# Attention with a sliding window and a spectral mix: v loaded like q and k and transposed twice, 128 keys per score tile

## The chip, the cores and the metric

The kernel runs on one core of a Trainium2 chip. It is timed on the device, in microseconds (us); a measurement is the median of several runs. Before the change it takes 463.44 us, the median of 3 runs (461.84 to 464.57). A profiled execution of the same kernel is where all views come from; its span is 460.1 us. The engines are called as the profile calls them: PE (TensorE, with PEld for its weight loads), DVE (VectorE), ACT (ScalarE), POOL (GpSimd) and SP (SyncE, which here issues transfers).

## The reference

Two stages follow each other. The first is attention for 8 batches, 8 heads, 576 tokens and 64 columns a head, with a window of 128 tokens and a bias that falls with the distance (one slope a head). The second takes the attention's output as `x` (8 x 576 x 512), multiplies the first 64 modes of its Fourier transform along the tokens by a complex 512 x 512 matrix each, and adds a product with `w_ch`.

```python
def _attn_ref(q, k, v):
    scores = scale * np.matmul(q, k.transpose(0, 1, 3, 2))
    rel = pos[:, None] - pos[None, :]
    bias = slopes[:, None, None] * (-np.abs(rel).astype(np.float32))[None, :, :]
    mask = (rel >= 0) & (rel < window)
    scores = np.where(mask, scores + bias[None], -1000000000.0)
    scores = scores - np.max(scores, axis=-1, keepdims=True)
    attn = np.exp(scores)
    attn = attn / (np.sum(attn, axis=-1, keepdims=True) + 1e-09)
    return np.matmul(attn, v)

def _moe_ref(x, w_r, w_i, w_ch):
    X = np.fft.rfft(x, axis=1)
    Y = np.zeros_like(X)
    Xr, Xi = (np.real(X[:, :n_modes]), np.imag(X[:, :n_modes]))
    Yr = np.einsum('bmd,mde->bme', Xr, w_r) - np.einsum('bmd,mde->bme', Xi, w_i)
    Yi = np.einsum('bmd,mde->bme', Xr, w_i) + np.einsum('bmd,mde->bme', Xi, w_r)
    Y[:, :n_modes] = Yr + 1j * Yi
    u = x + np.fft.irfft(Y, n=S, axis=1)
    return u + np.maximum(u @ w_ch, 0.0)
```

Everything comes and goes as float32; the kernel computes in bfloat16 with float32 sums. The weights `w_r` and `w_i` are 64 x 512 x 512 each, 134 MB in all.

## The kernel before

**Units and slots.** A unit is one pair of heads (`s`, 0 to 3) of one batch (`b`): 32 units. The first group is pair 0 of all batches (units 0 to 7), the second is pairs 1 to 3 (units 8 to 31). The order of work on every engine is the order in which the program writes it (a manual schedule). `_slot(n)` writes one slot: the scores of unit n, the transposes of unit n+1, the casts of units n+1 and n+2, the product with v of unit n-1 (`_av`) and the Fourier transform of unit n-2 (`_spectrum`, only after the last pair of a group: each slot in the first group, every third in the second). Slots 8 and later also hold modes (`_modes`): the weights' rows that belong to head pair 0 are multiplied while the attention of the other pairs runs. The rows of pairs 1 to 3 follow when all attention is done.

**Loads.** SP issues nearly all transfers in the program's order. `_load_unit` (L339) loads q and k of a unit: 128 partitions (two heads of 64), each with nine tokens in a row, 2,304 bytes. `_load_v` (L350) loads tokens 0 to 511 of v in two transfers, in rows of two tokens (512 bytes). `_load_vt` (L362) loads tokens 512 to 575 for all batches of a pair from POOL's queue; it and its cast `_cast_vt` run in slots 2 to 6 for pairs 1 to 3. q and k have nine buffers (`QK`), v six (`VB`). `_load_w` (L578) loads a tile of weights: three modes of pair 0, or one mode of pairs 1 to 3; there are three buffers (`RING`), so a tile's transfer is issued when the modes three tiles before it are done. Pair 0 has 22 tiles: three are loaded in advance, one more is issued per tile used.

**From q and k to scores.** POOL casts them to bfloat16 (L380). PE transposes them in 64x64 pieces, two heads at once in two corners of the array (L402, 18 matmuls for q, 18 for k), into one of two PSUM banks `tqk`. ACT copies a bank to SBUF in token order (L410, `qkT`). A score tile (`_score`, L419) holds in its upper 64 partitions 64 keys of one head and in its lower 64 the same keys of the other. As v comes in rows of two tokens, the even and the odd keys of 128 are two matmuls, r = 0 and 1, side by side in the bank:

```python
for r in range(2):
    for hh in range(2):
        hs = slice(64 * hh, 64 * hh + 64)
        nc.tensor.matmul(sc[hs, r * nq : (r + 1) * nq],
            lhsT=kT[hs, kt * P + r : kt * P + P : 2], rhs=qT[hs, kt * P : kt * P + nq], ...)
```

There are four tiles, `kt` 0 to 3, in two banks `sc` in turn: three of 512 columns and one of 448, which also holds the last 64 keys (L436). ACT takes the exponential (L440), DVE multiplies by the mask, which holds window and bias (L443, and L448 for the last tile).

**Product with v.** POOL casts v to `vb` (L391, four casts a unit). In `_av` 34 matmuls (L481) multiply 64 keys each by v and a column of ones, into the two banks of `av`; the two heads take the upper and the lower half of the array's rows. DVE divides by the sum that the ones gave (L487 to L493) and writes `x_sb`.

**Modes and what follows.** A mode is eight matmuls of 16 columns for pair 0 (L621 and L625); after eight modes ACT copies the sums out (L634, `ZTa`), and as there is one bank for them PE waits for it. After the attention, PE uses one tile of weights after another, and the transposes of x and its product with `w_ch` lie between them (`_xt`, `_xw`).

## Time and profile before

The table has each stage of the profiled execution (span 460.1 us): the time for which each engine was busy, the mean of the granted TensorE clock, and what the transfers moved.

| stretch, us | what runs | PE | DVE | ACT | POOL | clock | GB/s |
|---|---|---|---|---|---|---|---|
| 0 to 56 | constants, first group | 36.3 | 38.6 | 36.4 | 44.4 | 0.82 | 315 |
| 56 to 140 | second group, modes of pair 0 | 69.1 | 60.0 | 56.4 | 64.6 | 0.85 | 380 |
| 140 to 180 | its end | 33.7 | 23.4 | 19.8 | 15.8 | 0.76 | 379 |
| 180 to 224 | weights of pairs 1 to 3 | 27.6 | 13.7 | 10.2 | 2.2 | 0.62 | 396 |
| 224 to 410 | the same | 119.4 | 62.8 | 39.5 | 0.0 | 0.67 | 422 |
| 410 to 460 | inverse transform, output | 40.5 | 27.9 | 25.6 | 22.5 | 0.94 | 267 |

A busy time is the union of the engine's instructions in the stretch, so 69.1 of 84 us is 82% of the time. A line of a group in the profile reads: line of the kernel, engine, operation, tile written <- tiles read, shape, count | busy time, mean length of one in ns | idle time of the engine just before, and what ended it. A mean length contains the time until a result is there; the next instruction of the same engine often starts earlier. In a list of waits the figures are the sum, the count and the longest, in us. The chain of waits is followed back from the last instruction, each step to what released it. "issue" in both is time for which the profile shows no cause.

### The profile page before, as it was taken

What the parts mean: (1) busy time and instruction counts of PE and PEld (TensorE: products, weight loads), DVE (VectorE), ACT (ScalarE), POOL (GpSimd) and SP (SyncE); (2) the same over time, 40 slices, a digit from 0 to 9 for tenths busy, and PEclk for the clock granted to TensorE, in tenths of its full rate; (3) what the DMA queues carried; (4) which work ended last, traced back from release to release, by engine and by line L of the source; (5) the groups of instructions that cost most, each with busy time, mean ns of one, the idle gap of its engine ahead of it and who ended that gap; (6) DMA issues with size and microseconds to landing.
All of it is one profiled execution on the core that took longest, in us unless ns stands there. A gap on an engine that the chain in (4) does not pass through costs nothing.

```text
span 460.1 us, 14005 instructions
## 1 busy us (share of the span) xinstructions
PE 326.6 (71%) x5939; PEld 229.5 (50%) x5939; DVE 226.3 (49%) x492; ACT 187.9 (41%) x345; POOL 149.6 (33%) x255
## 2 busy tenths in 40 slices
PE   2778797797868985576646655566566578877994
PEld 2557576676757864343334433333333345534552
DVE  8776588658666572333323233133331334512884
ACT  3986576576664660223212122122221123412883
POOL 7697799677676522000000000000000000000882
PEclk9985689768895796566665577566655759979999
DMA  8999999999999999999999999999999999994697
GB/s 251 309 352 326 343 335 394 389 383 381 387 386 396 388 355 362 418 426 358 422 425 423 421 425 424 422 424 425 424 421 424 424 423 401 421 425 182 234 332 258
DMA packets 68382, 173.92 MB, mean 378 GB/s; under 512 B 5600, under 2 KB 21984, under 8 KB 68320
## 3 DMA queue, kind: packets, MB, share of 16 engines
q1 hardware_dynamic: 67936, 171.99, 96.9%
q0 software_dynamic: 384, 1.05, 0.9%
q8 instruction: 46, 0.75, 0.6%
q14 instruction: 16, 0.13, 0.1%
HBM read 163.58 MB, written 9.44 MB: 376 GB/s over the span
## 4 chain that ended last, share of the span: by engine, by line
DMA 48%; PE 32%; issue 6%; ACT 5%; DVE 3%; POOL 3%; SPq 2%; ACTq 0%; POOLq 0%; DVEq 0%
DMA wi<-in_moe_w_i_dram 42%; PE sc L428 6%; PE acc L625 4%; DMA v<-in_v_dram 4%; PE acc L621 4%; PE tqk L402 4%; PE av L481 3%; PE xt L523 3%; PE xw L669 2%; PE mm L656 2%; ACT qkT L410 1%; PE tp L647 1%; PE y L656 1%; SPq L345 1%; ACT hl L673 1%
## 5 line engine op out<-in xcount | busy, mean ns | idle before, releaser
L673 ACT CAST hl<-xw 64x512 bf16<-64x512 f32 x72 | 41.8, 580 | 165.2 <-PE xw L669 137.4
L625 PEld LDWEIGHTS <-wi 128*128 128x128 bf16 x1024 | 66.1, 104 | 79.6 <-DMA wi<-in_moe_w_i_dram 72.9
L795 POOL TENSOR_TENSOR o<-r,ys 128x512 f32<-128x512 f32 x18 | 22.5, 1277 | 247.1 <-DVE r L787 245.0
L625 PE MATMUL acc<-Xlast,wi 128*128 128x16 bf16 x768 | 56.0, 193 | 53.7 <-DMA wi<-in_moe_w_i_dram 53.7
L440 ACT ACTIVATE att<-sc 128x512 bf16<-128x512 f32 (+1 forms) x128 | 72.4, 592 | 45.2 <-PE sc L428 44.5
L621 PEld LDWEIGHTS <-wr 128*128 128x128 bf16 x1024 | 70.0, 106 | 41.9 <-DMA wr<-in_moe_w_r_dram 24.5
L674 DVE TENSOR_TENSOR hl<-xw,hl 64x512 bf16<-64x512 f32 x72 | 49.6, 689 | 83.2 <-ACT hl L673 83.1
L621 PE MATMUL acc<-Xlast,wr 128*128 128x16 bf16 x768 | 62.8, 194 | 21.7 <-DMA wr<-in_moe_w_r_dram 18.0
L391 POOL CAST vb<-v 64x256 bf16<-64x256 f32 x128 | 65.3, 510 | 28.8 <-PE av L481 19.4
L443 DVE TENSOR_TENSOR att<-att,mask 128x512 bf16<-128x512 bf16 x96 | 50.7, 556 | 31.2 <-ACT att L440 30.9
L428 PE MATMUL sc<-qkT,qkT 64*64 64x256 bf16 (+1 forms) x512 | 54.2, 325 | 12.5 <-ACT att L440 5.1
L669 PE MATMUL xw<-wch,xT 128*128 128x512 bf16 x144 | 60.1, 563 | 0.0
L649 DVE COPY xT<-tp 128x512 bf16<-128x512 bf16 x36 | 15.2, 423 | 58.3 <-PE tp L647 57.9
L410 ACT COPY qkT<-tqk 128x576 bf16<-128x576 bf16 x64 | 41.1, 644 | 4.9 <-PE tqk L402 4.9
L402 PE MATMUL tqk<-ident_b,qkb 64*64 64x64 bf16 x1152 | 33.1, 213 | 13.1 <-POOL qkb L380 8.7
L428 PEld LDWEIGHTS <-qkT 64*64 64x64 bf16 x512 | 31.5, 127 | 20.3 <-issue 11.3
L402 PEld LDWEIGHTS <-qkb 64*64 64x64 bf16 x1152 | 32.4, 129 | 15.4 <-POOL qkb L380 10.4
L481 PE MATMUL av<-vb,att 64*128 64x65 bf16 (+1 forms) x1024 | 31.8, 211 | 3.5 <-issue 3.5
L481 PEld LDWEIGHTS <-att 64*128 64x128 bf16 (+1 forms) x1088 | 26.7, 109 | 9.4 <-issue 5.9
L669 PEld LDWEIGHTS <-xT 128*128 128x128 bf16 x144 | 18.7, 135 | 21.6 <-issue 19.1
L380 POOL CAST qkb<-k 128x576 bf16<-128x576 f32 x32 | 26.1, 816 | 0.3 <-PE tqk L402 0.3
L380 POOL CAST qkb<-q 128x576 bf16<-128x576 f32 x32 | 23.7, 739 | 4.8 <-PE tqk L402 1.6
(107 smaller groups left out, 440.7 us busy)
## 6 DMA issues: line engine op xcount, KB each, us to landing
wr<-in_moe_w_r_dram SPq DMA_DIRECT2D x85, 768.0 KB, 8.3
wi<-in_moe_w_i_dram SPq DMA_DIRECT2D x85, 768.0 KB, 9.7
q<-in_q_dram SPq DMA_DIRECT2D x32, 288.0 KB, 7.2
k<-in_k_dram SPq DMA_DIRECT2D x32, 288.0 KB, 7.3
v<-in_v_dram SPq DMA_DIRECT2D x64, 128.0 KB, 6.5
out_dram<-o SPq DMA_DIRECT2D x32, 256.0 KB, 2.8
vt<-in_v_dram POOLq DMA_DIRECT2D x8, 128.0 KB, 7.2
wchf<-in_moe_w_ch_dram SPq DMA_DIRECT2D x2, 512.0 KB, 7.9
```

What stands on the lines that cost most here:

```text
L380: g.nc.gpsimd.tensor_copy(tb, t)
L391: g.nc.gpsimd.tensor_copy(o[64 * hh : 64 * hh + 64, i], u.v[64 * i : 64 * i + 64, hh])
L402: g.nc.tensor.transpose(tp[hs, r, :], u.b[w][hs, r], g.ident_b[hs, hs], tile_position=(64 * hh, 64 * hh))
L428: nc.tensor.matmul(sc[hs, r * nq : (r + 1) * nq], lhsT=kT[hs, kt * P + r : kt * P + P : 2], rhs=qT[hs, kt * P : kt * P + nq], start=True, ...
L440: nc.scalar.activation(a[:, :cols], sc[:, :cols], AF.Exp, scale=1.0 / math.sqrt(g.D))
L443: nc.vector.tensor_tensor(out=a, in0=a, in1=g.mask[:, s], op=ALU.mult)
L481: nc.tensor.matmul(av[o, hh, col(t)], lhsT=a[hs, c0 : c0 + m], rhs=vb[hs, 0 : D + 1], start=(j == 0), stop=(j == len(terms) - 1), tile_pos ...
L621: nc.tensor.matmul(o, lhsT=wr[:, a].bitcast(BF16)[:, 1::2][:, c], rhs=X[:, a, 1:3, :, m], start=(a == 0), stop=False)
L625: nc.tensor.matmul(o, lhsT=wi[:, a].bitcast(BF16)[:, 1::2][:, c], rhs=X[:, a, 0:2, :, m], start=False, stop=(a == A - 1))
L669: nc.tensor.matmul(xw, lhsT=xT[:, dt], rhs=g.wch[:, dt], start=(dt == 0 and g.way[n] != "q"), stop=(dt == 3))
L673: nc.scalar.copy(g.hl[hi, n, h], xw[hi])
L674: nc.vector.tensor_tensor(out=g.hl[lo, n, h], in0=xw[hi], in1=g.hl[hi, n, h], op=ALU.subtract)
```

## The change

v of all 576 tokens is loaded in one transfer of 2,304 bytes a row, as q and k are, and cast with them (`_cast`). PE transposes it in 64x64 pieces and ACT copies it to token order, as for q and k; then `_vnat` transposes it back in five pieces of 128 tokens by 128 columns (two heads), and DVE copies these to `vn`, beside a column of ones. So the keys are in order, and a score tile has 128 keys of one head on its 128 partitions: each of the two `sc` banks belongs to a head. The first two key tiles make a first pair of banks (`j` = 0), the other three a second (`j` = 1); the last of them, `kt` 4, takes keys 448 to 575 and queries 512 to 575. The masks are one of 512 columns for each of eight heads; for `j` = 0 its first 256 columns are used twice. The product with v sums over 128 keys in a matmul. The tail's loads, casts and buffers go, and so do the shorter mask and its slope tile. In the slot the second pair of scores comes after the first modes, v's first transposes after it and `_vnat` at the slot's end. The four masks of a unit are now multiplied before the division of the unit before. The diff, cut:

```diff
-                g.mask = cp.tile([P, NP, 512], BF16)
-                g.mask3 = cp.tile([P, NP, 448], BF16)
-                g.vbs = [cp.tile([P, 8, 72], BF16, name=f"vb{i}") for i in range(3)]
-                g.vbt = cp.tile([P, NP, B, 72], BF16)
+                g.mask = cp.tile([P, H, 512], BF16)
+                g.vns = [cp.tile([P, ST, 2, 72], BF16, name=f"vn{i}") for i in range(VN)]
                 g.qpool = actx.enter_context(tc.tile_pool(name="qk", bufs=QK))
                 g.vpool = actx.enter_context(tc.tile_pool(name="v", bufs=VB))
-                g.vts = actx.enter_context(tc.tile_pool(name="vts", bufs=2))
+                g.wcp = actx.enter_context(tc.tile_pool(name="wcp", bufs=1))
...
-                    _cast_qk(g, 0)
-                    for s in GROUPS[0]:
-                        _load_vt(g, s)
-                    _cast_qk(g, 1)
-                    _cast_v(g, 0)
-                    for s in GROUPS[0]:
-                        _cast_vt(g, s)
-                    _tr(g, 0, 0)
-                    _tr(g, 0, 1)
-                    _evac(g, 0, 0)
-                    _evac(g, 0, 1)
-                    first = dict.fromkeys(u[1] for u in units[:2])
+                    for n in range(2):
+                        _cast(g, n)
+                    for w in range(3):
+                        _tr(g, 0, w)
+                        _evac(g, 0, w)
+                    first = list(dict.fromkeys(u[1] for u in units[:2]))
                     rest = [s for s in range(NP) if s not in first]
                     for s in first:
-                        _mask(g, tp, s)
+                        _mask(g, s)
+                    _vnat(g, 0)
                     for n in range(3):
                         _slot(g, n, [], [])
                     for s in rest:
-                        _mask(g, tp, s)
+                        _mask(g, s)
...
-def _mask(g, tp, s):
...
+def _mask(g, s):
+
+    for h in (2 * s, 2 * s + 1):
+        g.nc.scalar.activation(g.mask[:, h], g.rel, AF.Exp, scale=-(2.0 ** (-8.0 * (h + 1) / g.H)))
...
+    u.v = g.vpool.tile([P, g.R, g.D], FP32, tag="v", name=f"v{n}")
+    g.nc.sync.dma_start(
+        out=u.v.rearrange("p r d -> p (r d)"),
+        in_=g.v[b, 2 * s : 2 * s + 2].rearrange("h (p r) d -> (h p) (r d)", r=g.R))
...
+def _cast(g, n):
     u = g.unit[n]
-    u.b = []
-    for w, t in enumerate((u.q, u.k)):
-        tb = g.work.tile([P, g.R, g.D], BF16, tag=f"qkb{w}", name=f"qkb{w}")
+    u.b, u.tp, u.T = [], [], []
+    for w, t in enumerate((u.q, u.k, u.v)):
+        tb = g.work.tile([P, g.R, g.D], BF16, tag=f"b{w}", name=f"b{w}")
         g.nc.gpsimd.tensor_copy(tb, t)
         u.b.append(tb)
 
 
-def _cast_v(g, n):
...
+def _start(t):
+
+    return t * P if t < 4 else 4 * P - 64
+
+
+def _vnat(g, n):
+
+    u = g.unit[n]
+    tp = g.ps1.tile([P, 10, 64], BF16, tag="tqk", name="tvn")
+    tp = tp.rearrange("p (t h) d -> p t h d", h=2)
+    for t in range(g.ST):
+        g.nc.tensor.transpose(
+            tp[:, t].rearrange("p h d -> p (h d)"),
+            u.T[2][:, _start(t) : _start(t) + P], g.ident_b)
+    u.vn = g.vns[n % VN]
+    g.nc.vector.tensor_copy(u.vn[:, :, :, 0 : g.D], tp)
+
+
+def _score(g, n, j):
 
 
     nc = g.nc
     u = g.unit[n]
     s = g.units[n][1]
-    qT, kT = u.qk
-    nq = 256 if kt < 3 else 192
-    cols = 512 if kt < 3 else 448
-    sc = g.ps1.tile([P, 512], FP32, tag="sc", name="sc")
-    for r in range(2):
+    qT, kT, _ = u.T
+    sc = [g.ps1.tile([P, 512], FP32, tag="sc", name="sc") for hh in range(2)]
+    parts = [(2 * j, 0, 256), (2 * j + 1, 256, 256)] if j == 0 else [(2, 0, 256), (3, 256, 192), (4, 448, 64)]
+    for kt, c0, nq in parts:
         for hh in range(2):
             hs = slice(64 * hh, 64 * hh + 64)
             nc.tensor.matmul(
-                sc[hs, r * nq : (r + 1) * nq],
-                lhsT=kT[hs, kt * P + r : kt * P + P : 2],
+                sc[hh][:, c0 : c0 + nq],
+                lhsT=kT[hs, _start(kt) : _start(kt) + P],
                 rhs=qT[hs, kt * P : kt * P + nq],
-                start=True, stop=True, tile_position=(64 * hh, 64 * hh))
-    if kt == 3:
-        for hh in range(2):
-            hs = slice(64 * hh, 64 * hh + 64)
-            nc.tensor.matmul(
-                sc[hs, 384:448], lhsT=kT[hs, 512:576], rhs=qT[hs, 512:576],
-                start=True, stop=True, tile_position=(64 * hh, 64 * hh))
-    a = g.work.tile([P, 512], BF16, tag=f"att{kt}", name=f"att{kt}")
-    nc.scalar.activation(a[:, :cols], sc[:, :cols], AF.Exp, scale=1.0 / math.sqrt(g.D))
-    u.att = getattr(u, "att", []) + [a]
-    if kt < 3:
-        nc.vector.tensor_tensor(out=a, in0=a, in1=g.mask[:, s], op=ALU.mult)
-
-
-def _mask3(g, n):
-    a = g.unit[n].att[3][:, 0:448]
-    g.nc.vector.tensor_tensor(out=a, in0=a, in1=g.mask3[:, g.units[n][1]], op=ALU.mult)
+                start=True, stop=True, tile_position=(64 * hh, 0))
+    u.att = getattr(u, "att", {})
+    for hh in range(2):
+        a = g.work.tile([P, 512], BF16, tag=f"att{j}{hh}", name=f"att{j}{hh}")
+        nc.scalar.activation(a, sc[hh], AF.Exp, scale=1.0 / math.sqrt(g.D))
+        u.att[j, hh] = a
+    for hh in range(2):
+        a, m = u.att[j, hh], g.mask[:, 2 * s + hh]
+        if j == 0:
+            a = a.rearrange("p (k q) -> p k q", k=2)
+            m = m[:, 0:256].unsqueeze(1).broadcast_to([P, 2, 256])
+        nc.vector.tensor_tensor(out=a, in0=a, in1=m, op=ALU.mult)
...
+        m = P if t < 4 else 64
         terms = []
-        for r in range(2):
-            if t > 0:
-                nq = 256 if t - 1 < 3 else 192
-                terms.append((att[t - 1], r * nq + P, P if t < 4 else 64, 2 * (t - 1) + r))
-            if t < 4:
-                nq = 256 if t < 3 else 192
-                terms.append((att[t], r * nq, P, 2 * t + r))
-        if t == 4:
-            terms.append((att[3], 384, 64, 8))
-        o = slice(0, P) if t < 4 else ps
-        for j, (a, c0, m, slot) in enumerate(terms):
-            vb = u.vb[:, slot] if slot < 8 else g.vbt[:, s, b]
-            for hh in range(2):
-                hs = slice(64 * hh, 64 * hh + 64)
+        if t > 0:
+            terms.append((t - 1, 256 * ((t - 1) % 2) + P))
+        terms.append((t, 256 * (t % 2) if t < 4 else 448))
+        o, kw = (slice(0, P), {}) if t < 4 else (ps, dict(tile_position=(0, po)))
+        for hh in range(2):
+            for i, (kt, c0) in enumerate(terms):
                 nc.tensor.matmul(
-                    av[o, hh, col(t)], lhsT=a[hs, c0 : c0 + m], rhs=vb[hs, 0 : D + 1],
-                    start=(j == 0), stop=(j == len(terms) - 1),
-                    tile_position=(64 * hh, 0 if t < 4 else po))
+                    av[o, hh, col(t)], lhsT=u.att[min(kt // 2, 1), hh][:, c0 : c0 + m],
+                    rhs=u.vn[:, kt, hh, 0 : D + 1],
+                    start=(i == 0), stop=(i == len(terms) - 1), **kw)
...
     N = len(g.units)
     if n < N:
         _score(g, n, 0)
-        _score(g, n, 1)
     if n + 1 < N:
         _tr(g, n + 1, 0)
         _evac(g, n + 1, 0)
         _tr(g, n + 1, 1)
+        _evac(g, n + 1, 1)
     for w in w0:
         _modes(g, *w)
     if n < N:
-        _score(g, n, 2)
+        _score(g, n, 1)
     if n + 1 < N:
-        _evac(g, n + 1, 1)
-    if n < N:
-        _score(g, n, 3)
+        _tr(g, n + 1, 2)
+        _evac(g, n + 1, 2)
     if n + 2 < N:
-        _cast_qk(g, n + 2)
-    if n + 1 < N:
-        _cast_v(g, n + 1)
-    for j, grp in enumerate(GROUPS[1:]):
-        for i, s in enumerate(grp):
-            if n == g.first[j + 1] - 4 + i:
-                _cast_vt(g, s)
-        for i, s in enumerate(grp):
-            if n == g.first[j + 1] - 6 + i:
-                _load_vt(g, s)
+        _cast(g, n + 2)
     if 0 <= n - 2 < N:
         _spectrum(g, n - 2)
     if 0 <= n - 1 < N:
         _av(g, n - 1)
-    if n < N:
-        _mask3(g, n)
     for w in w1:
         _modes(g, *w)
+    if n + 1 < N:
+        _vnat(g, n + 1)
```

## The prediction

> **What bounds the kernel now.** I read the page's slices first: they show where the transfers run at their best and where they do not.
>
> ```profile
> PE   2778797797868985576646655566566578877994
> ...
> PEclk9985689768895796566665577566655759979999
> DMA  8999999999999999999999999999999999994697
> GB/s 251 309 352 326 343 335 394 389 383 381 387 386 396 388 355 362 418 426 358 422 425 423 421 425 424 422 424 425 424 421 424 424 423 401 421 425 182 234 332 258
> ```
>
> A slice is 11.5 us. From slice 16 to 35 the DMA engines move some 424 GB/s and nothing else matters: that is the stream of weights. The attention fills the first 15 slices (to about 175 us); there the DMA engines are as busy but move only 250 to 395 GB/s, and TensorE is busy too. So the second view is the chain of waits in a stretch of the attention (60 to 140 us) and at its end (140 to 180), then what PE waited for in both.
>
> ```profile
> by line: PE sc L428 24.5%; issue 18.5%; PE av L481 13.2%; PE tqk L402 12.2%; PE xt L523 9.3%; PE acc L621 5.9%; ACT qkT L410 5.7%; PE acc L625 4.9%; ACT ZTa L634 2.3%; ACT att L440 2.2%; DVE X L534 0.9%; PE sc L436 0.6%; DVE X L535 0.4%; AC
> ```
>
> ```profile
> by line: DMA wi<-in_moe_w_i_dram 41.8%; PE sc L428 15.0%; PE tqk L402 10.8%; PE acc L621 8.6%; PE acc L625 7.1%; issue 6.9%; PE av L481 5.6%; PE xt L523 5.6%; ACT qkT L410 3.2%; ACT ZTa L634 1.5%; SPq L586 0.8%; PE sc L436 0.3%; ACT att L44
> ```
>
> PE's waits, 56 to 140 us:
>
> ```profile
> PE av L481 <- issue: 4.4, 4, 2.0
> PE tqk L402 <- issue: 2.5, 3, 1.2
> PE acc L621 <- ACT ZTa L634: 2.3, 3, 0.8
> PE sc L428 <- issue: 2.3, 1, 2.3
> PE acc L625 <- issue: 1.8, 1, 1.8
> ```
>
> PE's waits, 164 to 196 us:
>
> ```profile
> PE acc L625 <- DMA wi<-in_moe_w_i_dram: 7.1, 6, 1.7
> PE acc L621 <- DMA wr<-in_moe_w_r_dram: 2.9, 3, 1.5
> ```
>
> The reader is to see that no DMA stands in the chain from 60 to 140 us: PE's own bursts and "issue" make up nine tenths of it. The "issue" gaps come once in 256 PE instructions in the trace, just while a 16 KB packet of the instruction queue is on its way: PE waits for its code. From about 165 us PE waits for weights. The two limits therefore stand close together: the attention runs at PE's pace, and the moment it is over the transfers are already late.
>
> The granted clock and two groups give the prices (windows view, then groups by shape up to 190 us):
>
> ```profile
> 56.00:140.00 84.00, 69.06 (x1854) 58.84 (x1851) 60.00 (x149) 56.44 (x107) 64.61 (x111) 0.85 1.06 380
> ```
>
> ```profile
> L440 ACT ACTIVATE att<-sc 128x512 bf16<-128x512 f32 x96 | 54.2, 599 | 45.2 <-PE sc L428 44.5 <-DVE att L443 0.2
> L410 ACT COPY qkT<-tqk 128x576 bf16<-128x576 bf16 x64 | 41.1, 644 | 4.9 <-PE tqk L402 4.9
> L391 POOL CAST vb<-v 64x256 bf16<-64x256 f32 x128 | 65.3, 510 | 28.8 <-PE av L481 19.4 <-DMA v<-in_v_dram 3.7
> ```
>
> PE's own prices below are steps from one matmul's start to the next, read from the trace's start times, at full / half clock: transpose of 64x64 17/30 ns, score of 256 columns 71/102 and of 192 33/59 (two row halves run together), the product with v 20/33, a mode's matmul 32/32, a 128x128 transpose (L647) 56/92, a spectrum of 15 matmuls 1.5/2.3 us. From one tile shape to another (L402 to L621, L625 to L428, L436 to L481) a step is 122 to 152 ns.
>
> **The change, part by part.** *PE, one slot of the second group (24 slots).* Before: 12 scores of 256, 4 of 192, 2 of 64 (1.01/1.51 us), 36 transposes (0.61/1.08), 34 products (0.68/1.12), 19 of the 22 weight tiles in 24 slots (0.61), a spectrum every third slot (0.50/0.76), shape changes 0.40: 3.81/5.48. At 0.85 of the clock two thirds of the time are full: 1/(0.68/3.81+0.32/5.48) = 4.22, with 0.65 us of issue gaps (11.0 us in some 17 slots) 4.87. The trace has 72.5 us from the 9th to the 24th x_sb (L490), 4.83 a slot, so these prices hold. After: scores 6+2+2 (0.52/0.78, a saving), 54 transposes (0.92/1.62), five of 128x128 (0.28/0.46), 18 products over 128 keys at an estimated 33/54 ns (0.59/0.97), the same modes and spectrum, six or seven shape changes (0.78): 4.20/5.98, mean 4.64, with the gaps 5.29. That is +0.42 a slot. No row has a 128x128 product with 65 columns: a mode's 31 ns with 16 columns and L647's 92 ns bound it, -0.1 to +0.5 us a slot; I take 33/54, near the mode, whose weights are loaded alike. PE's instructions stay (11,880 to 11,816 rows), so the issue gaps do too.
>
> *ACT and a new wait.* One evacuation more (T of v), and it stands last in ACT's slot; `_vnat` waits for it and is PE's last of the slot, so the next slot's scores are queued behind it. Successive exponentials start 0.49 us apart, evacuations 0.52. From a slot's first score: 0.45 until its result, 2x0.49, 2x0.52, 2x0.49, 0.70 until T of v is seen = 4.15 us. PE at full clock is there after 0.28+0.08+0.61+0.12+0.77+0.12+0.25+0.08+0.31+0.13+0.59+0.13 = 3.47 us. Wait: 0.68 us, in the two thirds of slots without a spectrum and the two thirds of time at full clock: 0.3 a slot. Issue gaps take the place of part of it (-0.1), the ZTa copies come 0.52 us later behind one more evacuation in ACT's order, in 8 of 24 slots (+0.1). Sum +0.3; bounds 0 and 0.7.
>
> *DVE.* One copy from PSUM (640 elements; L649 takes 423 ns for 512, so 0.53) a unit, four masks of 512 in place of three and one of 448 (+0.08). It is ready 1.5 us after av, when PE has reached the second transposes of the next slot: covered, uncovered it would be up to 0.6 us. *POOL* casts 3 x 0.78 in place of 2 x 0.78 + 4 x 0.51 and issues no vt transfers (8 x 0.70 us): it is relieved by 1.3 us a unit, which PE's chain does not feel. *Constants:* two more 0.61 us exponentials after slot 2 against 2.9 us less on DVE ahead of the first mask, both under the wait for v below.
>
> *Transfers.* By the packet records, v's 16,384 packets of 512 B took 28.5 ns each (29.2 us on 16 engines), vt's 256 of 4 KB 263 ns (4.2 us). After: 4,096 of 2,304 B at q's and k's 102 ns (26.2 us). Saved: 7.2 us, at the share of 1.05 6.9 us. That is the most that the change can give, since the stream has no idle time to lose. SP issues 32 fewer. A sentence apart: the Trainium skill (DMA: Bandwidth & Descriptors, Specifications) has 512 B as the least size for full rate, by which v's packets would gain nothing and the most would be about 1 us; the trace has 18 B/ns at 512 B and 22.5 at 2,304, so it does not agree.
>
> *First group (to 61 us).* v is now cast a slot earlier, with q and k. v of unit 7 landed at 48.2 us and POOL waited 3.7 us for it; the saved vt packets and v packets before it (4.1 + 0.8 us) bring it to 43.5, so slot 6 gets to its av at about 45.5 (44.3 before), and three slots of 4.9 end at 60.2 against 60.7: -0.5, bounds -5 and +4.
>
> *Sum.* The attention's last av moves by -0.5 + 24 x (0.42 + 0.3) = +16.8 us. What follows swallows part: PE waited 10.0 us for weights from 164 to 196 and 1.7 more up to 224. If the attention is later, the ring's three tiles lie ready and these waits go; the 11.7 us are the cover. Beyond it the stream starts later. +16.8 - 11.7 = +5.1. On the profiled execution's 460.1 us span that is 465.2; the runs' median is 463.44, 3.3 above the span, so 468.5; I say 468.
>
> **Rivals.** *Compute keeps up, the transfers decide* (the other side). If a slot stays below about 5.0 us (wait for T of v hidden by the issue gaps, clock nearer to full), the attention moves by less than 5 us, the cover takes it all and the 6.9 us of packets are gained: 456.5. For it: at full clock alone PE's sum is only 0.39 us a slot more, and DVE's masks run faster beside a quieter POOL (409 ns the shortest, 528 busy on average). Against: the chain from 60 to 140 us has PE in it and no transfer. It decides at +5 us or less for the attention. *Swallowed:* slots of 5.2 to 5.4 us, +8 to +14, the cover eats it: 461 to 466. *The clock falls to half for the whole attention*, as 59 of 87 matmuls of a unit are transposes (36 of 88 before): slots of 5.98+0.65 = 6.6, 24 x 1.8 = +43 less 11.7: 494. Against it: 70 to 80 us, with a clock of 1.00 and transposes in it. The Trainium skill (TensorE: Matmul & The Clock Gate, Part 4: PE-mode transpose) says that transposes do not count as activity for the clock; this trace's full clock beside them bears that out only weakly.
>
> **How the numbers follow.** A measurement of this kernel tells 0.5% (2.3 us) from no change. Forecast, attention later than the cover: 0.54, its own range 466 to 480. Half clock 0.06. Swallowed 0.18. Transfers decide 0.22. Slower 0.60, same 0.18, faster 0.22. With the slots at +0.2 to +1.1 us the sum goes from the floor, 456.5, to 463.4 - 0.5 + 26.4 - 11.7 = 478; the range 456 to 480 leaves out the half clock and the ends.
>
> **What would show it.** Right: the starts of x_sb in the second group 5.3 to 5.9 us apart; PE waiting at `_vnat` for ACT's last evacuation; no wait for weights between 164 us and the end of the attention; DMA share below 1 from 70 to 180 us. Wrong: slots of 4.9 or less, or the clock at half throughout; and if PE still waits for weights at the end of the attention, the transfers decided.

## The result, and the profile after

The changed kernel takes 483.8 us (median of 4 runs, 478.81 to 486.5), against 462.64 us for the kernel before beside it. Two of the four runs (486.47 and 486.5) were in a slower state and are not in the ratio, which is 1.038 with a 95% interval of [1.032, 1.043]. The profiled execution has a span of 479.3 us against 460.1, so it is 19.2 us longer. The prediction had the sign right and the size wrong: 468 was forecast, and the measured time lies outside its range.

The page's slices of the changed kernel answer to the first ones shown of the kernel before; a slice is now 12.0 us:

```profile
PE   3877979779997899566665654664656559868995
...
PEclk9988686897669579657775566556556659988999
DMA  8999629999996979999999999999999999996587
GB/s 297 398 404 394 241 88 401 337 341 344 337 344 243 340 283 331 368 423 424 366 421 425 423 423 424 424 423 424 425 422 423 422 424 405 423 423 264 208 312 272
```

The stream of weights at some 424 GB/s now starts in slice 17 in place of 16 (counted from 0), after about 204 us in place of 184; it is as dense as before. What grew lies before it. DVE's last division (`x_sb`) marks the end of the attention. In the answers on that line the figures are the durations, then the first and the last start in us; the first row is the kernel before, the second the changed one:

```profile
L490 DVE TENSOR_TENSOR x_sb<-av,rec x3: 691/692/692, 167.7 to 173.5; 128x512 bf16<-128x512 f32 x3
```

```profile
L446 DVE TENSOR_TENSOR x_sb<-av,rec x3: 691/691/691, 189.3 to 195.3; 128x512 bf16<-128x512 f32 x3
```

So the attention ends 21.8 us later. The same line for the ninth unit stands at 64.8 us against 60.7: the first group lost 4.1 us, the second group 17.7 us (slots of 5.67 us against 4.90). In the stretch from 56 to 140 us (columns: PE, weight loads, DVE, ACT, POOL busy with their instructions, then clock, DMA share, GB/s) and in its chain of waits:

```profile
56.00:140.00 84.00, 72.82 (x1568) 55.92 (x1568) 59.10 (x143) 57.80 (x108) 34.57 (x46) 0.78 0.80 296
```

```profile
by line: PE tqk L353 16.6%; PE sc L397 10.2%; PE xt L479 8.7%; ACT att L405 7.5%; DVE att L412 7.3%; DVE x_sb L446 7.0%; PE av L437 6.2%; PE acc L567 4.9%; DVE vn L382 4.9%; PE tvn L378 4.9%; issue 4.5%; ACT T L361 3.9%; PE acc L571 3.7%; D
```

The transfers have room here: share 0.80 where it was 1.06. The chain, which was nine tenths PE and issue, now holds DVE's masks, division and copy (`vn`, L382) and ACT's exponentials and evacuations. PE's waits say why, in the same stretch:

```profile
PE tqk L353 <- DVE vn L382: 5.5, 9, 1.0
PE tvn L378 <- ACT T L361: 2.3, 6, 0.5
PE acc L567 <- ACT ZTa L580: 1.8, 2, 1.1
PE tqk L353 <- ACT T L361: 1.5, 2, 1.3
```

Not one "issue" gap is left among the large ones. The longest sum is a wait that the prediction had written off: PE's transposes of the next slot (L353) wait for DVE's copy of v out of PSUM. The order of time shows it for one slot, first on PE, then on DVE (start, duration; the view ends at 105.4, where 11 of the 18 last transposes had begun):

```profile
103.66 0.45 PE L378 MATMUL tvn<-ident_b,T 128*128 128x128 bf16 x5 [0.54 <-ACT T L361]
104.04 0.39 PE L397 MATMUL sc<-T,T 64*128 64x256 bf16 x4
104.36 0.47 PE L353 MATMUL tqk<-ident_b,b 64*64 64x64 bf16 x18
105.24 0.35 PE L353 MATMUL tqk<-ident_b,b 64*64 64x64 bf16 x11 [0.40 <-DVE vn L382]
```

```profile
102.61 1.14 DVE L412 TENSOR_TENSOR att<-att,mask 128x512 bf16<-128x512 bf16 x2 [1.40 <-ACT att L405]
103.68 0.20 DVE L443 RECIPROCAL rec<-av 128x8 f32<-128x8 f32 x1
103.91 0.69 DVE L446 TENSOR_TENSOR x_sb<-av,rec 128x512 bf16<-128x512 f32 x1
104.52 0.27 DVE L449 TENSOR_TENSOR x<-av,rec 64x128 bf16<-64x128 f32 x1
104.71 0.47 DVE L382 COPY vn<-tvn 128x640 bf16<-128x640 bf16 x1
```

`_vnat` (L378) waits 0.54 us for ACT's T of v. Its result is complete at 104.1, but DVE has the division of the unit before first (here behind the second pair of masks, which end at 103.75) and copies only at 104.71. As `tqk` has two banks, the transposes of k of the next unit need the bank that `_vnat` filled: 0.40 us more. After them come, in order, the modes, the second scores, the transposes of v, ACT's T of v, and the next `_vnat`. This is a loop through three engines, a slot long.

At the end of the attention PE waits for weights as before (160 to 245 us):

```profile
PE acc L571 <- DMA wi<-in_moe_w_i_dram: 7.0, 7, 1.7
...
PE acc L567 <- DMA wr<-in_moe_w_r_dram: 2.8, 3, 1.1
```

That is 9.8 us where 11.7 stood. The waits went along with the attention.

### The profile page after: what moved, and what is told of

The parts are those of the page before. It is cut to its first block, busy times and chain, and to the rows that moved or that the text cites. A ratio compares the mean times of both kernels' runs of the same rounds, so it can differ in the third digit from the quotient of the medians.

```text
span 479.3 us, 13884 instructions
## 1 busy us (share of the span) xinstructions
PE 350.6 (73%) x5879; PEld 240.3 (50%) x5907; DVE 242.3 (51%) x508; ACT 207.2 (43%) x377; POOL 101.5 (21%) x144
## 4 chain that ended last, share of the span: by engine, by line
DMA 40%; PE 31%; DVE 14%; ACT 10%; issue 4%; SPq 1%; POOL 0%; ACTq 0%; DVEq 0%; POOLq 0%
DMA wi<-in_moe_w_i_dram 38%; PE tqk L353 5%; ACT att L405 4%; PE acc L571 4%; PE sc L397 4%; PE acc L567 4%; PE xt L479 3%; PE av L437 3%; DVE x_sb L446 2%; ACT T L361 2%; DVE att L412 2%; PE tvn L378 2%; PE xw L615 2%; PE mm L602 2%; DMA out_dram<-o 1%
## 5 line engine op out<-in xcount | busy, mean ns | idle before, releaser
L405 ACT ACTIVATE att<-sc 128x512 bf16<-128x512 f32 x128 | 70.2, 605 | 52.7 <-PE sc L397 52.6
L353 PE MATMUL tqk<-ident_b,b 64*64 64x64 bf16 x1728 | 53.0, 214 | 19.5 <-DVE vn L382 9.2
L361 ACT COPY T<-tqk 128x576 bf16<-128x576 bf16 x96 | 60.5, 659 | 2.6 <-PE tqk L353 2.5
L353 PEld LDWEIGHTS <-b 64*64 64x64 bf16 x1728 | 43.7, 127 | 35.5 <-issue 25.8
L595 DVE COPY xT<-tp 128x512 bf16<-128x512 bf16 x36 | 15.2, 423 | 55.8 <-PE tp L593 55.5
L342 POOL CAST b<-q 128x576 bf16<-128x576 f32 x32 | 23.2, 726 | 63.4 <-PE tqk L353 55.5
L397 PE MATMUL sc<-T,T 64*128 64x256 bf16 (+2 forms) x320 | 33.4, 303 | 2.2 <-ACT att L405 1.9
L437 PE MATMUL av<-vn,att 128*128 128x65 bf16 (+1 forms) x576 | 33.5, 217 | 0.5 <-DVE x L449 0.5
L342 POOL CAST b<-v 128x576 bf16<-128x576 f32 x32 | 24.4, 761 | 28.4 <-PE tqk L353 12.5
L437 PEld LDWEIGHTS <-att 128*128 128x128 bf16 (+1 forms) x576 | 27.5, 115 | 5.0 <-issue 0.6
L342 POOL CAST b<-k 128x576 bf16<-128x576 f32 x32 | 25.5, 796 | 8.5 <-PE tqk L353 6.2
L378 PE MATMUL tvn<-ident_b,T 128*128 128x128 bf16 x160 | 18.9, 267 | 7.5 <-ACT T L361 7.2
```

The costliest lines, as they stand in the source:

```text
L342: g.nc.gpsimd.tensor_copy(tb, t)
L353: g.nc.tensor.transpose(tp[hs, r, :], u.b[w][hs, r], g.ident_b[hs, hs], tile_position=(64 * hh, 64 * hh))
L361: g.nc.scalar.copy(dst.rearrange("c (p r) -> c p r", r=g.R), u.tp[w][:, 0 : g.R].rearrange("c r p -> c p r"))
L397: nc.tensor.matmul(sc[hh][:, c0 : c0 + nq], lhsT=kT[hs, _start(kt) : _start(kt) + P], rhs=qT[hs, kt * P : kt * P + nq], start=True, stop=T ...
L405: nc.scalar.activation(a, sc[hh], AF.Exp, scale=1.0 / math.sqrt(g.D))
L437: nc.tensor.matmul(av[o, hh, col(t)], lhsT=u.att[min(kt // 2, 1), hh][:, c0 : c0 + m], rhs=u.vn[:, kt, hh, 0 : D + 1], start=(i == 0), sto ...
```

## The experiments

Three questions: which wait sets the slot; what the parts of the change are worth; why nothing behind the attention took up the delay. Every time is a median, every ratio is to the kernel before on the same chip. "Rest" is the span less the start of the last `x_sb`; "tiles" are the weight tiles issued by then.

| version | us | ratio | last x_sb | slot, second group | clock there | rest | tiles |
|---|---|---|---|---|---|---|---|
| before | 463 | 1 | 173.5 | 4.90 | 0.82 | 286.6 | 22 |
| after | 483.8 | 1.038 [1.032, 1.043] | 195.3 | 5.67 | 0.78 | 284.0 | 22 |
| e1 | 470.06 | 1.015 [1.010, 1.020] | 181.7 | 5.17 | 0.81 | 286.8 | 22 |
| e2 | 450.39 | 0.973 [0.968, 0.978] | 163.4 | 4.58 | 0.84 | 283.7 | 22 |
| e3 | 484.26 | 1.048 [1.043, 1.053] | 197.2 | 5.84 | 0.75 | 285.4 | 22 |
| e5 | 473.82 | 1.020 [1.013, 1.028] | 185.0 | 5.46 | 0.86 | 287.8 | 22 |
| e6 | 474.12 | 1.025 [1.019, 1.030] | 184.2 | 5.24 | 0.84 | 286.5 | 22 |
| e7 | 461.79 | 0.999 [0.996, 1.001] | 175.6 | 5.10 | 0.89 | 285.0 | 22 |
| e8 | 474.9 | 1.021 [1.014, 1.029] | 187.2 | 5.36 | 0.68 | 286.8 | 22 |
| e9 | 483.75 | 1.047 [1.041, 1.052] | 201.8 | 5.99 | 0.71 | 278.5 | 25 |
| e10 | 485.92 | 1.047 [1.042, 1.053] | 198.1 | 5.90 | 0.69 | 287.0 | 22 |
| e11 | 474.63 | 1.026 [1.019, 1.032] | 190.4 | 5.58 | 0.75 | 288.5 | 22 |
| e12 | 463.69 | 1.000 [0.996, 1.004] | 175.5 | 5.07 | 0.84 | 286.3 | 22 |
| e13 | 459.77 | 0.989 [0.985, 0.994] | 179.3 | 5.27 | 0.77 | 278.9 | 24 |
| e14 | 482.16 | 1.041 [1.037, 1.045] | 192.9 | 5.67 | 0.86 | 285.5 | 22 |
| e15 | 474.79 | 1.023 [1.018, 1.028] | 186.3 | 5.37 | 0.89 | 287.0 | 22 |
| e16 | 472.97 | 1.020 [1.016, 1.025] | 180.1 | 5.21 | 0.94 | 287.8 | 22 |
| e17 | 461.49 | 0.997 [0.994, 1.000] | 180.9 | 5.25 | 0.79 | 278.6 | 24 |

The time is a median, and the last five columns come from the one profiled execution. For e11 that was the longest of its four (480.76 us, the others 474.3 to 474.9), for e16 the shortest (469.67), and these columns are to be read so.

### e1: v's second transposes half a slot later

```diff
     if n < N:
+        _vnat(g, n)
         _score(g, n, 1)
...
-    if n + 1 < N:
-        _vnat(g, n + 1)
```

> The changed kernel with the second transposes of v (and DVE's copy of them) moved into the middle of the next slot, where T of v has long been ready and the copy stands before the division. Its attention is 21.8 us later than before the change. Theory A (PE's own time and its changes of tile shape make the slot longer; the waits for ACT and DVE only took the place of the issue gaps): the waits of 12.6 us in the second group go, most of their time comes back as issue gaps, 0 to -5 us, 478 to 484. Theory B (the waits for T of v and for the copy make the slot longer): -12 to -17 us, 464 to 470.

Three fifths of the loss went (1.038 to 1.015). The waits for the copy are no longer among PE's large ones (for 5.7 us from 56 to 140 us, and some 14 us over both groups, it now waits for ACT ahead of `_vnat`), and the work of PE is the same, instruction for instruction. So most of the loss was not work but where the work stands.

### e2: no transposes of v

```diff
-    for w, t in enumerate((u.q, u.k, u.v)):
+    u.vn = g.vns[n % VN]
+    g.nc.gpsimd.tensor_copy(
+        u.vn.rearrange("p t h c -> p (t h) c")[:, 0 : g.R, 0 : g.D], u.v)
+    for w, t in enumerate((u.q, u.k)):
...
-    if n + 1 < N:
-        _tr(g, n + 1, 2)
-        _evac(g, n + 1, 2)
...
-    if n + 1 < N:
-        _vnat(g, n + 1)
```

> The changed kernel without any transposes of v: POOL casts v straight into the buffer of the products, which leaves out putting the keys of v in order; scores, masks and products of 128 keys stay. Theory A: a unit loses 18 + 5 transposes, one evacuation, one copy and two or three changes of shape, about 1.0 us of PE, 31 us in all; the attention ends some 9 us earlier than before the change and the transfers limit: 455 to 463. Rival (the 128-key scores and products are what costs): still above 472.

This version leaves out the ordering of the keys, so what it computes is not the attention; it is a measure of the parts only (`vn` also has four buffers in place of two). Scores and products over 128 keys, with one wide load of v, are by themselves a gain of 2.7%, more than expected. Then the transfers are near their limit; the stretch from 56 to 140 us of e2 has a DMA share of 0.99:

```profile
56.00:140.00 84.00, 67.92 (x1527) 51.20 (x1527) 59.65 (x156) 59.18 (x112) 39.16 (x56) 0.84 0.99 383
```

### e3 and e6: scores in quarters

```diff
-            nc.tensor.matmul(
-                sc[hh][:, c0 : c0 + nq],
-                lhsT=kT[hs, _start(kt) : _start(kt) + P],
...
+            for c in (0, 64):
+                nc.tensor.matmul(
+                    sc[hh][c : c + 64, c0 : c0 + nq],
+                    lhsT=kT[hs, _start(kt) + c : _start(kt) + c + 64],
...
+                    start=True, stop=True, tile_position=(64 * hh, c))
```

Each score is made by two matmuls of 64 keys, in the array shape that the transposes have, so that PE need not change its shape between them. e3 does it in the changed kernel.

> The changed kernel with each score matmul cut into two of 64 keys, so that scores use the same 64x64 corners of the array as the transposes: 10 more matmuls a unit, no change of shape between scores and transposes. Theory A (shape changes): two steps a slot fall from 0.27 and 0.18 us to 0.08, -0.29 us a slot, -9 us: 475. Rival (the number of PE instructions and their fetch count): 11% more instructions, 0 to +5 us: 484 to 489.

The step from a score to the transposes fell from 214 to 101 ns, 4.1 us over the second group, and the time did not fall. What PE saved it spent waiting for the same copy, 7.3 us in place of 5.5; e3's first two waits on PE from 56 to 140 us:

```profile
PE tqk L353 <- DVE vn L382: 7.3, 10, 1.1
PE tvn L378 <- ACT T L361: 3.6, 6, 1.0
```

e6 does it together with e1, where the copy is out of the way:

> The changed kernel with both edits: v's second transposes in the middle of the next slot (470 alone) and scores in quarters (no gain alone). Theory B (the chain over ACT and DVE set the slot, so PE's saving on changes of shape was lost in a longer wait; with the chain cut it counts): -4 to -8 us against 470, 462 to 466. Rival (the quarters' 10 extra matmuls a unit cost as much as the shape changes): 469 to 475.

1.025 against 1.015: no gain here either. In the profiled executions the time without PE's waits falls, from 4.60 to 4.38 us a slot, and the waits grow by more (13.0 to 19.8 us in the second group): those for ACT ahead of `_vnat` from 4.9 to 6.3 us, the "issue" gaps from 0.9 to 6.7 us. The change of shape is a real cost, but quarters did not recover it.

### e5: eight idle matmuls a unit in the kernel before

```diff
+    if n >= g.first[1]:
+        for i in range(8):
+            nc.tensor.matmul(
+                av[:, 0, 384:512], lhsT=g.ident_b, rhs=g.ident_b, start=True, stop=True)
     avv = av[:, :, 0 : ST * (D + 1)].rearrange("p h (t c) -> p h t c", t=ST)
```

> The kernel before the change, with eight idle 128x128 matmuls of 128 columns more in every product with v of the second group: 24 x 8 x 56 to 92 ns, 11 to 18 us of PE. As predicted (PE's waits for weights after the attention swallow 11.7 us): 463 to 467. Rival (the last tiles of weights are issued only when the ring's buffers come free, so the waits move along with the attention): +10 to +15 us, 473 to 478.

The profiled attention ends 11.5 us later and the span is 12.7 us longer. If 11.7 us of cover existed, the kernel should hardly have noticed. It noticed all of it, 10.3 us in the median.

### e7: v's second transposes behind the first ones of the next unit

```diff
     if n + 1 < N:
         _tr(g, n + 1, 2)
         _evac(g, n + 1, 2)
+    if n < N:
+        _vnat(g, n)
...
-    if n + 1 < N:
-        _vnat(g, n + 1)
```

T of v was evacuated most of a slot earlier, and DVE's copy comes ahead of the division, because `_av` comes later in the slot.

> The changed kernel with v's second transposes of unit n in slot n, behind the first transposes of v of the next unit, so that their PSUM bank has long been copied out; in the middle of the slot PE waited 13.9 us for that bank. Theory B: these waits go, a part comes back as a wait for DVE's copy at the next slot's transposes: 462 to 468. Rival (the wait only changes its place, or issue gaps take it): 468 to 474.

The whole loss is gone: 0.999 [0.996, 1.001]. In PE's waits of e7 from 56 to 140 us the copy is not among the first, and the "issue" gaps, which the prediction read as waits for code, are back, as in the kernel before; below them the stretch itself:

```profile
PE tqk L352 <- issue: 5.6, 5, 2.1
PE acc L566 <- ACT ZTa L579: 3.9, 3, 1.4
PE tqk L352 <- ACT T L360: 1.4, 3, 1.1
```

```profile
56.00:140.00 84.00, 71.14 (x1772) 57.06 (x1772) 65.56 (x158) 63.47 (x120) 35.27 (x51) 0.94 0.94 352
```

In the same 84 us PE does 13% more instructions (1772 against 1568) at a clock of 0.94.

### e8: v loaded in the order of keys

```diff
+    for hh in range(2):
+        g.nc.sync.dma_start(
+            out=u.v[:, 0:4, hh],
+            in_=g.v[b, 2 * s + hh, 0:512].rearrange("(t p) d -> p t d", p=P))
     g.nc.sync.dma_start(
-        out=u.v.rearrange("p r d -> p (r d)"),
-        in_=g.v[b, 2 * s : 2 * s + 2].rearrange("h (p r) d -> (h p) (r d)", r=g.R))
+        out=u.v[:, 4], in_=g.v[b, 2 * s : 2 * s + 2, 448:576].rearrange("h p d -> p h d"))
```

The other way to have keys in order: rows of one token (256 bytes), and no transposes of v.

> The kernel without transposes of v (450 with the keys of v left unordered), with v loaded in the order of the keys, in rows of 256 bytes: 1,280 packets a unit for 128 of 2,304 bytes. That kernel is limited by its transfers (DMA share 0.99 from 56 to 140 us). If a packet has a fixed part of some 9 ns as the small ones show and 19 ns in all: +22 us, 468 to 474. If packets cost by their bytes alone (11 ns): 450 to 455.

The opposite price: PE has as little work as in e2, and now waits for what the transfers bring. From 64 to 188 us it waits 7.0 us for POOL's casts and 10.0 us for weights, and POOL itself waits 39.5 us for v. A packet of 256 bytes took 18.6 ns, as the first theory had it. Short rows cost more than e2 gains, 2.1% over the kernel before.

### e10 and e11: which of the two waits

e10 issues the second transposes of a unit at the end of its own slot, so that T of v is long there, while DVE's copy still stands behind the division. e11 leaves `_vnat` where the change has it, and puts the division behind the copy in DVE's order.

```diff
-    if n + 1 < N:
-        _vnat(g, n + 1)
+    if n < N:
+        _vnat(g, n)
```

> The changed kernel with v's second transposes still at the end of PE's slot and the copy still behind the division, but of unit n in slot n: their T was copied out a slot earlier, so PE does not wait for ACT there. If the wait for T of v is the main part of the loss: 467 to 473. If the wait for DVE's copy, which the next slot's second transposes meet, is the main part: 476 to 482.

```diff
-    if 0 <= n - 1 < N:
-        _av(g, n - 1)
+    divide = _av(g, n - 1) if 0 <= n - 1 < N else None
...
         _vnat(g, n + 1)
+    if divide:
+        divide()
```

> The changed kernel with the division of the product moved behind DVE's copy of v, all PE work in its place: the copy no longer stands behind 1 us of division, the wait for T of v stays. If the copy is the main part of the loss: 468 to 474. If the wait for T is: 477 to 483.

PE's first waits, 60 to 198 us of e10 and 62 to 191 us of e11:

```profile
PE tqk L352 <- DVE vn L381: 7.7, 12, 1.5
PE acc L566 <- ACT ZTa L579: 4.7, 5, 1.3
```

```profile
PE tvn L378 <- ACT T L361: 6.9, 10, 0.9
PE acc L577 <- ACT ZTa L590: 5.7, 5, 1.4
```

With the wait for T alone taken away nothing is won (1.047): the copy's wait is there, with 7.7 us. With the copy's wait alone taken away a part is won (1.026), and the wait for T grows from 3.8 to 6.9 us. Two stations of one loop; the whole gain came only where both were out of the way, in e7.

### e14, e15 and e16: is it the clock?

In the versions with the longest slots the granted clock is low (0.78 after, 0.69 in e10, 0.89 in e7), so that a low clock could be a cause by itself. Five transposes of the identity, into the bank that the real ones then overwrite, fill PE's wait ahead of `_vnat`: in the changed kernel (e14), in e11 (e15), and in e7, which has no wait at that place (e16).

```diff
     for t in range(g.ST):
+        g.nc.tensor.transpose(
+            tp[:, t].rearrange("p h d -> p (h d)"), g.ident_b, g.ident_b)
+    for t in range(g.ST):
         g.nc.tensor.transpose(
```

> The changed kernel, with five 128x128 transposes of the identity into the bank of the second transposes of v, ahead of the real ones, which overwrite them. They need nothing but the bank, so they run where PE waits for ACT's T of v. Theory E (the granted clock falls because PE stands still): the mean clock from 56 to 140 us rises from 0.78 to 0.84 or more and the slots of the second group get shorter than 5.67 us in spite of the added work, 474 to 481 us. Theory W (the clock is no part of it, the waits alone set the slot): the clock stays within 0.03 of 0.78; the added 0.29 to 0.5 us a slot less the 0.16 us of wait that they fill is 3 to 8 us, so 484 to 489.

> The same five transposes in the version with the division behind the copy, whose wait for T of v at that place is the longest, 6.8 us in the second group (0.3 us a slot). Theory E: the clock from 56 to 140 us rises by 0.05 or more and the slots fall below 5.45 us, under 472 us against 474.6. Theory W: the five transposes are about hidden by the wait (0 to 0.2 us a slot left over), clock within 0.03 of what it was, 474 to 479.

> The same five transposes in the version with the second transposes right after v's first ones of the next unit, where PE has no wait to fill. Both theories: 0.29 to 0.45 us a slot more, 7 to 11 us in the second group, and as much in the end if nothing after the attention takes it up: 467 to 473 against 461.8. This is the price of the five alone, to hold against the two versions in which a wait covers them.

The stretch from 56 to 140 us of e14, then PE's first wait in it:

```profile
56.00:140.00 84.00, 74.48 (x1671) 58.40 (x1667) 60.42 (x145) 57.74 (x109) 33.61 (x47) 0.86 0.82 307
```

```profile
PE tqk L353 <- DVE vn L385: 4.8, 9, 0.9
```

Both theories were half right. The clock rises when PE has more to do: from 56 to 140 us 0.78 to 0.86 in e14, and from 0.88 to 0.93 in e15. Over the whole execution it is 0.765 to 0.778 in all four of e14 and 0.721 to 0.759 in all four of the changed kernel. But the time does not fall: e14 takes 1.041 [1.037, 1.045] against 1.038, with slots of 5.67 us as before, and e15 1.023 against 1.026 for e11.

That does not mean that the clock is worth nothing. The next table adds up PE's waits over 0.15 us in the second group, from the ninth start of `x_sb` to the last (23 slots); PE's own time is what is left of a slot.

| version | slot, us | PE's waits, us | PE's own time a slot, us | clock |
|---|---|---|---|---|
| before | 4.90 | 17.7 | 4.13 | 0.82 |
| after | 5.67 | 17.1 | 4.93 | 0.78 |
| e1 | 5.17 | 13.0 | 4.60 | 0.81 |
| e7 | 5.10 | 15.8 | 4.42 | 0.89 |
| e10 | 5.90 | 15.2 | 5.24 | 0.69 |
| e11 | 5.58 | 15.7 | 4.90 | 0.75 |
| e14 | 5.67 | 15.0 | 5.02 | 0.86 |
| e16 | 5.21 | 17.0 | 4.47 | 0.94 |

In e14 the five transposes take 9.0 us of the second group, read from start to start without the wait among them, but the waits fall by only 2.1 us and the group is as long as before (130.5 us). So PE's other work took some 7 us less, at the higher clock, and that paid for most of the added work. In e16, where no wait covers the same five, they take 6.9 us, and the kernel is 2.1% slower than e7 (1.020 against 0.999). No run raises the clock without adding work, so what a higher clock alone would bring is not shown.

The table also says what the gain of e7 consists of. The waits for T of v, for DVE's copy and for a bank that ACT copies T from were 12.1 us and are 2.6, but 6.1 us of "issue" gaps come in their place, and the waits for the copy of the sums (`ZTa`) grow from 4.5 to 5.8. Of the 13.1 us that e7's second group is shorter, 11.8 are PE's own time, with the same instructions at a clock of 0.89 in place of 0.78. So it is shown that the place of `_vnat` and of the copy makes the loss. How much of it is the wait itself, and how much the lower clock that went with it, is not separated; nor is it shown why the clock differs so much when the waits' sum hardly does.

### e9, e13 and e17: the weights used earlier

```diff
-SHARE, SHARE_END = 4, 7
+SHARE, SHARE_END = 6, 4
...
-TAIL = 2
+TAIL = 0
```

These constants say how many steps of pair 0's modes a slot takes, and how many slots after the attention remain for them. e9 is the changed kernel with these:

> The changed kernel with pair 0's weight tiles used earlier: more modes in the slots up to 23, fewer in the last ten, none after the last product. Ring theory (the last tiles are used faster than three buffers and 8 us of landing allow, so PE waits for weights after the attention however late it ends): the waits of 7.4 us shrink, -3 to -8 us, 474 to 480 (fast runs 472 to 477). Rival (the stream of weights itself is late): within 2 us of the changed kernel.

The waits for weights at the end of the attention halved (9.8 to 5.1 us from 160 to 245 us), the rest became 5.5 us shorter, and the attention 6.5 us longer. The time, 483.75 us, is what the rival had forecast, but not for the rival's reason, so by time alone it decides nothing. e12 is e7 with ACT's evacuation of k behind the first modes, meant to bring the copy of the sums (`ZTa`) forward:

```diff
-        _evac(g, n + 1, 1)
     for w in w0:
         _modes(g, *w)
+    if n + 1 < N:
+        _evac(g, n + 1, 1)
```

> The best version so far (v's second transposes behind the first ones of the next unit, 461.8) with ACT's copy of k's transposes after the first modes, so that the copy of the modes' sums, for which PE waits 5.9 us in the second group, comes one evacuation earlier. If that wait counts: -2 to -4 us, 458 to 460. If transfers or PE's other work take it: 461 to 463.

No gain, 1.000 [0.996, 1.004]. e13 is e12 with `SHARE, SHARE_END` 5, 6 and `TAIL` 1; e17 is the kernel before with these constants and nothing else.

> The same with pair 0's weights used a little earlier (shares 5 and 6, one slot of tail), so that the last tiles are not used faster than they land. If the weights' ring sets the end: -2 to -4 us against the run beside it. If attention gets longer by what is gained, as with the changed kernel: within 1 us of it.

> The kernel before with the tiles of pair 0 used earlier (five and six a slot in place of four and seven, one slot after the attention in place of two), nothing else. Theory R (what lies behind the attention is fixed by the number of tiles issued by its end): 24 tiles are issued by the last division in place of 22, the stretch from there to the end falls from 286.6 to 278 to 281 us, the attention grows by 1 to 4 us, and the kernel takes 456 to 461. Rival (weights wait for something else at that point): the stretch stays at 284 us or more and the time within 0.5% of the kernel before.

The last two columns of the first table answer the third question. In all fifteen versions with the old constants 22 tiles are issued by the last `x_sb`, and the rest takes 283.7 to 288.5 us, whatever the attention took (163 to 198 us). Of 86 tiles 64 are then left, and 64 x 1.57 MB / 423 GB/s = 238 us, with the inverse transform and the output behind them. With 24 tiles issued the rest takes 278.6 and 278.9: two tiles less to move are 2 x 1.57 MB / 423 GB/s = 7.4 us. (e9, with 25, has 278.5, no less; but in e13 and e17 one of the two transfers of the 25th tile is issued by then too.) e17's attention grew by 7.4 us, where 1 to 4 were expected, so little of it is left (0.997). e13 has the same constants on top of the better placement; at 0.989 [0.985, 0.994] it is 1.1% faster than the kernel before, 3.9 us below e12, as its first theory had it.

## Why the prediction was right in the sign and wrong in the size

**The sum for the second group came out right by luck.** Forecast were 0.72 us a slot and 17.3 us; measured are 0.77 and 17.7. The forecast was made of +0.42 for PE's own time and +0.3 for waits. In the trace PE's own time per slot went from 4.13 to 4.93 us, and the waits did not grow in sum (17.7 us in the second group of the kernel before, 17.1 now): the "issue" gaps (12.5 us) vanished, where the prediction had them stay, and the new waits took their place. For the own time the forecast had 4.22 to 4.64 at a clock of 0.85; its own prices at the granted 0.78 give 1/(0.56/4.20 + 0.44/5.98) = 4.83. The product over 128 keys was the unknown, and its step was priced well: 31/54 ns in the trace, 33/54 estimated. The burst of 18 comes to 38/63 ns, because a change of tile shape lies in it, from 128x128 to 128x64.

**"Covered, uncovered it would be up to 0.6 us"** is the first step that failed. The prediction set the copy's readiness 1.5 us after the products and PE's second transposes after that. In the 20 slots of the second group where the order is plain, the copy ends 1.6 to 2.5 us after the last product, 2.0 in the middle. It stands behind 1.0 to 1.5 us of division, which begins as the products end or, as in the slot shown, up to 0.6 us later. But PE is done with the transposes ahead of the bank 1.1 us after the last product in the quickest slots, and the prediction's own prices at full clock made it 1.2 (0.13 + 0.28 + 0.13 + 0.28 + 0.08 + 0.31), less than its 1.5. In the slot shown PE was there 0.40 us too early. The prediction had named the bank's user and DVE's position without following them round to the next slot. The step named as the new wait, ACT's T of v, is real (3.8 us in the second group, where 0.3 a slot or 7 were forecast), but it is one half of a loop. e7, e10 and e11 show that the gain asks for both halves.

**"-0.5" for the first group** is the second. It held that v's landing paces slot 6. After the change PE does not wait for v there; it waits for the copy (2.3 us) and for T of v (1.3 us). The first `x_sb` starts 1.3 us later, the slots take 5.47 us against 5.12, and the group ends 4.1 us later. In e7, with the same transfers, the ninth `x_sb` starts at 58.2 us against 60.7 before the change: this loss too comes from the place of `_vnat`.

**"The 11.7 us are the cover"** is the third, and the one that made the number wrong. The forecast subtracted all of it; 2.6 us were swallowed (21.8 less 19.2). Of the 14.1 us between the 465.2 of the forecast and the 479.3 measured, 9.1 are this step, 4.6 the first group and 0.4 the second. e5 shows it with nothing else changed: an attention 11.5 us longer made the kernel 12.7 us longer. PE waits for weights there because it uses the last tiles of pair 0 faster than three buffers let them come: each transfer's issue waits for the use of the tile three before, and lands 7 to 8 us later. So the waits belong to the end of the attention and move with it. SP's own waits, over the whole execution, show the tie in the changed kernel (`SPq` is its queue):

```profile
SPq L532 <- PE acc L571: 179.4, 65, 5.9
SPq L532 <- PE sc L397: 60.3, 14, 15.8
```

Had -11.7 been -2.6 and -0.5 been +4.1, the same sum, with the second group's 17.3, would give 460.1 + 4.1 + 17.3 - 2.6 = 478.9, where 479.3 was measured. The 6.9 us of saved packets came free, as forecast (share 0.80), and were of no use, since in that stretch the weights wait for the ring.

**The rivals.** "Transfers decide" needed an attention within 5 us of the old one, which the changed kernel did not have. e7 has it (2.1 us later) and takes 461.8 us, not 456.5: the rest of the kernel (285.0 us against 286.6) hangs on the tiles, and the saved packets did not shorten it by 6.9 us. "Swallowed" fell with the cover. "Half clock" did not come: 0.78 in the second group, and added work raised it. The prediction beside it cited the Trainium skill (TensorE: Matmul & The Clock Gate, Part 4: PE-mode transpose), that transposes do not count as activity. The runs say otherwise, if these transposes run in the mode that the Trainium skill means there (the trace calls them MATMUL like the rest): the five added in e14 are transposes alone, and the clock rose from 0.78 to 0.86.

**What was to show it.** Slots of 5.3 to 5.9 us (5.67), the wait at `_vnat` and the share below 1 came as said. "No wait for weights between 164 us and the end of the attention" did not, and the text gave the wrong reading for that case: the transfers had not decided (share 0.80); the ring had moved, as e5 and e17 show.

## What to carry to other kernels

Before a wait at the end of a stage is counted as cover, ask what releases it: if a ring ties the transfer to the stage's own progress, the wait moves along, and the end of the stage plus a constant is the end of the kernel. When a change adds a stop on a shared buffer, follow the buffer round to its next user and write down what stands ahead of the release in that engine's order; two short waits on two engines can be one loop, where taking one away only feeds the other. An operand that several engines hand on should be started where its buffer is long free and its copy stands ahead of the long work, which here was worth the whole loss without one instruction fewer. And before a wait is called the loss, take PE's waits and its own time apart: here their sum changed little from version to version, and the own time, with the clock in it, carried most of the difference.

## What the runs showed of the hardware that was not expected

- Idle work raises the clock: five extra transposes a slot brought the stretch from 56 to 140 us from 0.78 to 0.86 (e14), and the longest single wait listed there for the changed kernel was 1.3 us. What they cost was for the most part won back by PE's other work at the higher clock (9.0 us added, 2.1 us of waits filled, the same length). The Trainium skill (TensorE: Matmul & The Clock Gate, A second HAM failure mode: psum-queue depth-cycling) says that short standstills between groups of matmuls make the clock oscillate; these runs agree.
- A change of the array's shape has unequal prices. From the last score (64x128) to the first transpose (64x64) a step takes 214 ns on average in the changed kernel, where it took 80 ns between scores and transposes of the kernel before, both in 64x64; from transposes to the 128x128 products 148 ns.
- The "issue" gaps are not a fixed toll: 12.5 us in the second group of the kernel before, none of note in the changed one, 6.1 us in e7. They come at every 256th PE instruction. The packet of 16 KB of the instruction queue, which the prediction saw on its way just then, had landed up to 0.9 us before the gap in nine of the twelve of the kernel before (60 to 175 us). But in all twelve PE went on 2.2 to 2.5 us after the packet's start, and at none of the 54 places of this kind in these three kernels did it go on sooner than 2.2 us. That fits a wait for code, which shows only where PE runs ahead without other waits.
